# RWKV-6 and a tanh-shrink layer: the own scores of six blocks move from TensorE to VectorE, and the last tile's copies to another buffer

## The chip, the cores and the metric

The kernel runs on one core of one Trainium2 chip. A core has a matrix engine (TensorE, PE in the profile), an elementwise and reduction engine (VectorE, DVE), an engine for scaled copies and functions of one operand (ScalarE, ACT), a general engine (GpSimd, POOL) and a queue that issues most transfers (SyncE, SP). They run side by side, each in its own order, and wait for one another by semaphores. TensorE reads the on-chip memory (SBUF) and writes only PSUM, the small accumulator memory.

The metric is the device time of one execution in microseconds (us). Before the change it is 591.21 us, the median of three runs (590.17 to 591.8).

## The reference

Two layers follow each other. The first is a recurrence over tokens, for each of 4 batches and 8 heads with 48 channels a head and 768 tokens:

```python
for t in range(S):
    kt, vt, rt, wt = (k[:, :, t], v[:, :, t], r[:, :, t], w[:, :, t])
    cur = np.einsum('bhd,bhe->bhde', u[None] * kt, vt)
    y[:, :, t] = np.einsum('bhd,bhde->bhe', rt, state + cur)
    state = wt[:, :, :, None] * state + np.einsum('bhd,bhe->bhde', kt, vt)
```

The second takes the result as x of 3072 rows and 384 columns:

```python
h = x @ w_in            # 384 -> 2048
g = h - np.tanh(h)
return (g @ w_out).astype(np.float32)   # 2048 -> 384
```

What matters here is the part `cur`: token t also sees itself, through the sum over the 48 channels d of r[t,d] u[d] k[t,d], one number for each token and head. This is called the own score of the token. Everything is fp32.

## The kernel before, in words

The 3072 tokens are cut into 8 blocks of 384 tokens (two halves of each batch). The eight heads of a block are four pairs, and two heads lie on the 128 partitions, 64 partitions each of which 48 hold channels. In time a block is cut into six chunks of 64 tokens. Within a chunk, the recurrence becomes matmuls: a 64x64 matrix of scores for each head and chunk, in which the entry (s, t) is what token t takes from token s. Entries with s < t come from k times the decay behind s ("post") and r times the decay before t ("pre"); this phase is `earlier`. Entries with s = t are the own scores; this phase is `own`. Both call `gram`, which makes 48 matmuls of 64x64 for a block (each is two passes in fp32, so 96 rows in the trace), and a masked copy, L406 `copy_predicated`, takes the wanted entries from PSUM into the matrix A (named scores in the profile), twice per phase and block. `own` uses k multiplied by u: `times_u` (L364) does this on ScalarE, four operations a block.

The other phases of a block are: `turn` (transposes), `update` (`update_1` on TensorE makes the contributions of each chunk to the state, `update_2` adds them up on VectorE, ten or eleven small operations at L459 and L469), and the result, in which `from_states` (L510) multiplies pre with the states and `from_scores` (L527) multiplies the scores with v. Scratch in PSUM is a pool of two buffers, `ps_a`, that all phases share; the result takes both.

While the dense layer of block i runs, the phases of block i+1 ("later") are spread over it, and the first scans of block i+2 ("after"). The dense part is a loop over f, 16 slices of 128 of the 2048 inner columns. In each slot f:

- `first` makes hp, six TensorE passes (L668) into a single PSUM buffer, and ScalarE copies it to h (L671).
- `slight` makes g from h. In blocks 2 to 6 ("fast") ScalarE squares (L686, L687, L689) and VectorE does two products (L674). In the other blocks VectorE also does the square (L695).
- `second.add` does the matmuls with w_out. In blocks 2 to 6 it is the class `Fewer` (L775), which multiplies 3x3 tiles with fewer products and needs sums of tiles of g, made on VectorE by `form_g` (L713): one operation in the slot after an even f, four after an odd one. It also needs sums of tiles of w_out, made once by `form_w` (L951): the first half under block 1, the second half under block 2, in slots 4, 6, 8 and 9. The matmuls of slices f-1 and f follow two and three slots after an odd f. Twelve sums (L807) then give the output tiles of a fast block, under the next block, in slots 4, 6, 8 and 9, and `store` sends them off in slot 9, six transfers. In the other blocks the second matmuls are L743.

The order on TensorE, VectorE, ScalarE and SyncE is written out by hand (`manual_schedule`): the order in which the program issues operations is the order on each engine. In a slot, VectorE gets the products of the slot before, the copies of the phase issued in the slot before, the forms, then what the plan prepares, then the weight forms and sums. `plan(i)` is the table of what goes into which slot: `phases` (TensorE phases), `before` (preparations for the later block: `times_behind` L353, `times_before` L346, `held`, `times_u`, `bound`), `ahead` (preparations for the block after: the scans `behind` L339 and `before` L328), and `loads`. A load is tied by `begin_behind` to the copy of h of its slot, and all loads, the stores and the fills of xT go through SyncE's one queue in order. k, r, w and v have one buffer each, which the next load of the same name overwrites.

At the end, the last tile of 128 rows is copied in two halves, by ScalarE and VectorE (L751, L753), into the pool buffer o, which has two buffers used by the two tiles before it (L758), and each half is stored by its own queue.

The table that the change rewrites is this one, for all blocks but block 0:

```python
phases = {4: "own", 6: "earlier", 8: "turn", 10: "update", 12: "result 1"}
...
before.update({4: ("bound 2",), 6: ("bound 0",)})
ahead = {10: ("behind 2", "take_whole 2"), 12: ("behind 0", "take_whole 0"), 13: ("before 2",),
         15: ("before 0",)}
loads = {1: "v", 7: "w", 9: "k", 11: "r"}
```

Of the kernel before, what the change touches and what calls it, by code (L numbers as in the profile page):

```python
# [37 lines left out]
F32 = mybir.dt.float32  # L38
# [13 lines left out]
P = 128  # L52
# [66 lines left out]
def kernel(  # L119
# [4 lines left out]
    wT: bass.AP,  # L124
    v: bass.AP,
    uT: bass.AP,
    weights: bass.AP,
    out: bass.AP,
):
# [12 lines left out]
        nc.vector.memset(shift[:, i:i + 1], value)  # L142
    u_sb = const.tile([P, NPAIR], F32, name="u_sb", tag="u_sb")
    nc.scalar.dma_start(out=u_sb, in_=uT)

    warm = const.tile([P, 1], F32, name="warm", tag="warm")
    nc.scalar.activation(out=warm, in_=shift[:, 0:1], func=AF.Copy)


    seed = const.tile([P, UP * NCH * LP], BF16, name="seed", tag="seed")  # L150
    nc.vector.memset(seed, 0.0)
    nc.vector.memset(seed.rearrange("d (c j) -> d c j", j=LP)[:, :, 0:1], 1.0)


    start = const.tile([P, UP * NCH * LP], F32, name="start", tag="start")
# [66 lines left out]
    fast = range(2, blocks_n - 1)  # L222
    n_whole = blocks_n * NPAIR * NCH
    n_excess, n_top = 2 * blocks_n + len(fast) * NF, (blocks_n - len(fast)) * NF
    holds = const.tile([P, n_whole + n_excess + n_top], F32, name="holds", tag="holds")
    ends = const.tile([P, 3], F32, name="ends", tag="ends")
    excess = const.tile([P, n_excess], F32, name="excess", tag="excess")
    top = const.tile([P, n_top], F32, name="top", tag="top")
# [33 lines left out]
    class Block:  # L262
# [40 lines left out]
        def load(self, name, p0=0, n=NPAIR, as_=None):  # L303
            as_ = as_ or name
            if name == "w":
                dst = self.tile(name)[:, p0 * NCH * LP:(p0 + n) * NCH * LP]
                src = wT[self.b, p0:p0 + n, :, self.q * NCH * LP:(self.q + 1) * NCH * LP]
            else:
                dst = self.tokens(as_, p0, n)
                src = {"r": rT, "k": kT}[name][self.b, p0:p0 + n, :, self.cols]  # L310
            return nc.sync.dma_start(out=dst.rearrange("d (p t) -> d p t", p=n),
                                     in_=src.rearrange("p d t -> d p t"))

        def load_v(self):
            self.v = inp.tile([P, NCP, DM], F32, name="v_sb", tag="v_sb")
# [419 lines left out]
    class Second:  # L735
# [4 lines left out]
        def add(self, f, g):  # L740
            for j in range(NB // P):
                acc = self.acc[j][:, 0:DM]
                nc.tensor.matmul(acc, lhsT=g[:, j * P:(j + 1) * P], rhs=w_out_sb[:, f, :],  # L743
                                 start=(f == 0), stop=(f == NF - 1))
                if f == NF - 1:
                    rows = slice(self.row0 + j * P, self.row0 + j * P + P)
                    if rows.stop == N:
                        for at, engine in ((slice(0, DM // 2), nc.scalar), (slice(DM // 2, DM), nc.vector)):
                            o = dense.tile([P, DM], F32, name="o", tag="o", bufs=2)[:, at]
                            if engine is nc.scalar:  # L750
                                nc.scalar.activation(out=o, in_=acc[:, at], func=AF.Copy, scale=1.0 / UPSCALE)  # L751
                            else:
                                nc.vector.tensor_single_scalar(o, acc[:, at], 1.0 / UPSCALE, op=ALU.mult)  # L753
                            queue = nc.scalar if engine is nc.scalar else nc.sync
                            queue.dma_start(out=out[rows, at], in_=o)
                        continue
                    o = dense.tile([P, DM], F32, name="o", tag="o", bufs=2) if j < 2 else places(12, 3)
                    nc.scalar.activation(out=o, in_=acc, func=AF.Copy, scale=1.0 / UPSCALE)  # L758
                    nc.sync.dma_start(out=out[rows, :], in_=o)
# [57 lines left out]
    def plan(i):  # L817


        converted = ()  # L820
        if i == 0:
            phases = {4: "turn", 6: "update", 8: "own", 11: "earlier", 13: "result 1"}
            before = {0: ("behind 0", "take_whole 0"), 1: ("times_behind 2",), 2: ("times_behind 0",),
                      3: ("before 2",), 4: ("times_u 2",), 5: ("before 0", "times_u 0"), 8: ("times_before", "held")}
            ahead = {14: ("behind 2", "take_whole 2"), 15: ("behind 0", "take_whole 0")}
            converted = range(READY, NF)
            loads = {f: "weights" for f in (0, 1, 3, 4, 5, 6, 7, 8, 9, 10)}
            loads.update({2: "v", 11: "w", 12: "k", 13: "r"})
        else:
            phases = {4: "own", 6: "earlier", 8: "turn", 10: "update", 12: "result 1"}  # L830
            if i == 1:
                before = {0: ("before 2",), 1: ("before 0",), 2: ("times_behind 2", "times_behind 0"),
                          3: ("times_before", "held", "times_u 2", "times_u 0")}
            else:
                before = {0: ("times_behind 2",), 1: ("times_behind 0", "times_u 2"),
                          3: ("times_before", "held", "times_u 0")}
            before.update({4: ("bound 2",), 6: ("bound 0",)})
            ahead = {10: ("behind 2", "take_whole 2"), 12: ("behind 0", "take_whole 0"), 13: ("before 2",),
                     15: ("before 0",)}
            loads = {1: "v", 7: "w", 9: "k", 11: "r"}  # L840
        return phases, before, ahead, converted, loads

    READY = 3
# [5 lines left out]
    def more_weights(queue):  # L849
        raws.append(load_weights(more_weights.n, queue))  # L850
        more_weights.n += 1
        return raws[-1][-1]
# [7 lines left out]
    def boot(ps, blk, later):  # L860
        h1, h2 = HALVES
        for p0 in HALVES:
            for name in ("w", "k", "r"):
                blk.load(name, p0, UP)
        blk.load_v()
        for _ in range(3):
            more_weights(nc.sync)
        ready = []

        def converted():  # L870
            for op in ready.pop(0):
                op()

        both = (h1, h1 + 1), (h2, h2 + 1)
        blk.behind(h1, UP)
        blk.take_whole(h1, UP)
        blk.before(h1, UP)
        blk.times_behind(h1, UP)
        blk.times_u(h1, UP)
        blk.turn(ps, h1)  # L880
        own = blk.own(ps, h1)
        blk.times_before(h1, UP)
        earlier = blk.earlier(ps, h1)
        blk.bound(h1)
        blk.bound(h2)
        blk.behind(h2, UP)
        blk.take_whole(h2, UP)
        blk.times_behind(h2, UP)
        blk.times_u(h2, UP)
        blk.turn(ps, h2)  # L890
        ins = blk.before(h2, UP)
        begin_behind(ins, later.load("w"))
        own()
        own = blk.own(ps, h2)
        blk.times_before(h2, UP)
        earlier()
        blk.update_1(ps)
        own()
        ready.append(convert(*raws.pop(0), halves=True))
        blk.results(ps)  # L900
        blk.result("from_scores", both[0])
        blk.update_2()
        ready.append(convert(*raws.pop(0)))
        later.bound(h1)
        blk.result("from_states", ALL, cs=(0, 1), more=True)
        earlier = blk.earlier(ps, h2)
        blk.result("from_states", ALL, cs=(2,))
        earlier()
        blk.result_out(both[0], True)
        later.bound(h2)  # L910
        blk.fill_holes([nc.sync, nc.scalar, nc.gpsimd])
        more_weights(nc.sync)
        blk.result("from_scores", both[1], True)
        for op in ready[0][0]:
            op()
        ins = blk.result_out(both[1], True, (nc.scalar.copy, nc.vector.tensor_copy))
        begin_behind(ins, more_weights(nc.sync))
        more_weights(nc.sync)
        later.load("k")
        later.load("r")  # L920
        blk.held(0, NPAIR)
        ready[0] = ready[0][1]
        converted()
        ready.append(convert(*raws.pop(0)))
        converted()
        later.prepare("behind 2")
        later.prepare("take_whole 2")
        converted()
# [24 lines left out]
    for i, blk in enumerate(blocks):  # L953
# [14 lines left out]
        for f in range(NF):  # L968
# [29 lines left out]
                    after.prepare(name)  # L998
            if fast and i == 1 and f >= 5 and f - 5 < len(W_FORMS):
                form_w(f - 5, 0)  # L1000
            some = {4: (0, 2), 6: (2, 4), 8: (4, 6), 9: (6, len(SUMS))}.get(f)
            if some and i == fast.start and fast:
                for n in range(some[0], min(some[1], len(W_FORMS))):
                    form_w(n, 4)
            if some and summed:
                summed[0].sum(*some)
                if f == 9:
                    summed.pop().store()
            name, ins = loads.get(f), None
            if name == "weights":  # L1010
                ins = more_weights(nc.sync)
            elif name == "v":
                ins = later.load_v() if later else None
            elif name and after:
                ins = after.load(name)
# [90 lines left out]
```

## Time and profile before

| | |
|---|---|
| median of three runs | 591.21 us (590.17 to 591.8) |
| the profiled execution | 591.68 us, of which the span of the profile is 589.9 us |
| granted TensorE clock | 0.989 |
| VectorE forms L713, 128x256 | 200 operations, 84.8 us, 424 ns each |
| masked copies L406, 128x768 | 32 operations, 30.5 us, 1,005 ns each |
| weight forms L951, 128x512 | 20 operations, 683 to 685 ns each |
| times_before L346, 128x1536 | 7 operations, 1,752 ns each |
| own matmuls L399, r with k | 768 passes over 8 blocks |
| scaling by u, L364 on ScalarE | 32 operations, 17.7 us |
| loads of v, 576 KB | 8, median 4.4 us from issue to landing |
| HBM traffic | 69 GB/s over the span |

The profile is taken of one execution. [...] The chain that ended last is followed back from the last instruction: it says what the end waited for, step by step. A wait is named after what released it. [...]

### The profile page before, as it was taken

What the parts mean: (1) busy time and instruction counts of PE and PEld (TensorE: products, weight loads), DVE (VectorE), ACT (ScalarE), POOL (GpSimd) and SP (SyncE); (2) the same over time, 40 slices, a digit from 0 to 9 for tenths busy, and PEclk for the clock granted to TensorE, in tenths of its full rate; (3) what the DMA queues carried; (4) which work ended last, traced back from release to release, by engine and by line L of the source; (5) the groups of instructions that cost most, each with busy time, mean ns of one, the idle gap of its engine ahead of it and who ended that gap; (6) DMA issues with size and microseconds to landing.
All of it is one profiled execution on the core that took longest, in us unless ns stands there. A gap on an engine that the chain in (4) does not pass through costs nothing.

```text
span 589.9 us, 14756 instructions
## 1 busy us (share of the span) xinstructions
PE 562.6 (95%) x6130; PEld 405.3 (69%) x6130; DVE 455.9 (77%) x906; ACT 343.6 (58%) x689; POOL 10.9 (2%) x39
## 2 busy tenths in 40 slices
PE   3689999999999999999999999999999999999995
PEld 2546656566665787777777787777877787775552
DVE  8899996875877888887887888877888886554541
ACT  4789874343137665587467765686566875532221
POOL 6000000000000000000000000000000000000000
PEclk9789999999999999999999999999999999999998
DMA  8495543202302032011311033011321001000101
GB/s 316 120 388 181 166 159 117 80 2 58 105 12 82 2 109 61 6 42 55 106 56 42 2 96 108 12 42 36 115 66 34 10 1 42 12 1 0 42 1 43
DMA packets 27655, 43.17 MB, mean 73 GB/s; under 512 B 2368, under 2 KB 25536, under 8 KB 27584
## 3 DMA queue, kind: packets, MB, share of 16 engines
q1 hardware_dynamic: 27168, 41.98, 22.0%
q8 instruction: 49, 0.80, 0.6%
q14 instruction: 22, 0.18, 0.1%
q10 hardware_dynamic: 352, 0.15, 0.1%
q0 software_dynamic: 64, 0.05, 0.0%
HBM read 36.28 MB, written 4.72 MB: 69 GB/s over the span
## 4 chain that ended last, share of the span: by engine, by line
PE 89%; DVE 3%; ACT 2%; issue 1%; DMA 0%; DVEq 0%; ACTq 0%
PE hp L668 40%; PE acc L775 19%; PE acc L743 14%; PE att L775 5%; PE att L399 3%; PE att L510 2%; PE att L447 2%; PE att L527 2%; PE att L422 2%; DVE w_sb L251 0%; DVE states L459 0%; ACT up L246 0%; DMA out_y<-o 0%; ACT up L247 0%; DVE states L469 0%
## 5 line engine op out<-in xcount | busy, mean ns | idle before, releaser
L668 PE MATMUL hp<-xT,w_sb 128*128 128x384 f32 x768 | 272.0, 491 | 5.5 <-ACT h L671 3.0
L668 PEld LDWEIGHTS hp<-xT,w_sb 128*128 128x128 f32 x768 | 140.0, 191 | 88.5 <-ACT h L671 7.3
L671 ACT ACTIVATE h<-hp 128x384 f32<-128x384 f32 x128 | 62.7, 490 | 169.6 <-PE hp L668 167.9
L775 PE MATMUL acc<-forms,g 128*128 128x128 f32 x720 | 108.4, 278 | 0.6
L775 PEld LDWEIGHTS acc<-forms,g 128*128 128x128 f32 x720 | 96.2, 192 | 12.8 <-issue 1.2
L713 DVE TENSOR_TENSOR g<-g 128x256 f32<-128x256 f32 x200 | 84.8, 424 | 17.4 <-PE acc L775 1.1
L674 DVE SCALAR_TENSOR_TENSOR h<-h,s 128x384 f32<-128x384 f32 x128 | 70.6, 552 | 25.4 <-ACT s L686 24.9
L674 DVE SCALAR_TENSOR_TENSOR g<-qa,h 128x384 f32<-128x384 f32 x96 | 53.6, 559 | 19.7 <-PE acc L775 8.6
L743 PE MATMUL acc<-w_sb,sums 128*128 128x384 f32 x192 | 68.0, 490 | 0.2
L695 DVE CUSTOM_DVE_ANT_0 s<-h 128x384 f32<-128x384 f32 x48 | 26.7, 555 | 38.3 <-ACT h L671 38.3
L743 PEld LDWEIGHTS acc<-w_sb,sums 128*128 128x128 f32 x192 | 35.7, 190 | 23.7 <-issue 0.5
L687 ACT ACTIVATE qa<-s,shift 128x384 f32<-128x384 f32 x80 | 49.2, 615 | 2.6
L689 ACT ACTIVATE junk<-s,shift 128x384 bf16<-128x384 f32 x80 | 47.9, 599 | 0.0
L686 ACT ACTIVATE s<-h 128x384 f32<-128x384 f32 x80 | 41.9, 524 | 2.5
L698 ACT ACTIVATE qa<-s,shift 128x384 f32<-128x384 f32 x48 | 29.5, 614 | 23.9 <-DVE top L695 23.9
L775 PE MATMUL acc<-w_sb,g 128*128 128x128 f32 x240 | 39.9, 275 | 0.0
L743 PE MATMUL acc<-w_sb,g 128*128 128x384 f32 x96 | 33.3, 487 | 0.0
L775 PEld LDWEIGHTS acc<-w_sb,g 128*128 128x128 f32 x240 | 33.2, 192 | 0.0
L406 DVE COPY_PREDICATED scores<-mask_all,att 128x768 f32<-128x768 uint8 x32 | 30.5, 1005 | 1.4 <-PE att L399 1.4
L328 DVE TENSOR_TENSOR_SCAN pre<-w,start 128x780 f32<-128x780 f32 x16 | 28.6, 1786 | 0.6
L339 DVE TENSOR_TENSOR_SCAN post<-w,seed 128x780 f32<-128x780 f32 x16 | 28.4, 1776 | 0.0
L775 PE MATMUL att<-w_sb,g 128*128 128x128 f32 x160 | 26.8, 275 | 0.0
(80 smaller groups left out, 537.7 us busy)
## 6 DMA issues: line engine op xcount, KB each, us to landing
raw<-in_weights SPq DMA_DIRECT2D x16, 768.0 KB, 5.2
w<-in_wT SPq DMA_DIRECT2D x7, 780.0 KB, 4.4
k<-in_kT SPq DMA_DIRECT2D x7, 768.0 KB, 4.7
r<-in_rT SPq DMA_DIRECT2D x7, 768.0 KB, 4.6
v_sb<-in_v SPq DMA_DIRECT2D x8, 576.0 KB, 4.4
out_y<-sums SPq DMA_DIRECT2D x15, 128.0 KB, 1.9
out_y<-o SPq DMA_DIRECT2D x6, 192.0 KB, 2.5
xT<-late SPq DMA_DIRECT2D x44, 24.0 KB, 1.9
```

Of the source, the lines that this page charges most:

```text
L328: return nc.vector.tensor_tensor_scan(out=self.tile("pre")[:, cols], data0=self.tile("w")[:, cols], data1=start[:, 0:n * NCH * LP], initia ...
L406: return lambda: nc.vector.copy_predicated(out=A[:, :, p0:p0 + UP].rearrange("s h p c t -> s h (p c) t"), mask=mask.to_broadcast([P, 2, UP ...
L668: nc.tensor.matmul(hp, lhsT=w_in_sb[:, f, kc, :], rhs=xT[kc], start=(kc == KC - 1), stop=(kc == 0))
L671: return h, nc.scalar.activation(out=h, in_=hp, func=AF.Copy, scale=1.0 / UPSCALE)
L674: return lambda: nc.vector.scalar_tensor_tensor(out=out, in0=in0, scalar=scalar, in1=in1, op0=op0, op1=ALU.mult)
L686: nc.scalar.activation(out=s, in_=h, func=AF.Square)
L687: nc.scalar.activation(out=qa, in_=s, func=AF.Square, bias=shift[:, 4:5])
L689: nc.scalar.activation(out=junk[:, 0:NB], in_=s, func=AF.Relu, bias=shift[:, 5:6], accum_out=excess[:, at:at + 1])
L698: first = [lambda: nc.scalar.activation(out=qa, in_=s, func=AF.Square, bias=shift[:, 4:5])]
L713: return lambda: nc.vector.tensor_tensor(out=G[:, to:to + 2], in0=two(G, g_at(q, a0), g_at(q, a1)), in1=two(G, g_at(q, b0), g_at(q, b1)), ...
L743: nc.tensor.matmul(acc, lhsT=g[:, j * P:(j + 1) * P], rhs=w_out_sb[:, f, :], start=(f == 0), stop=(f == NF - 1))
L775: nc.tensor.matmul(to, lhsT=G[:, g_at(q, a), :], rhs=rhs, start=start, stop=stop, skip_group_check=True)
```

## The change

Three things are changed.

First, in the phases of blocks 2 to 7 (those that run under the dense part of blocks 1 to 6) the own phase is gone, and with it `times_u`. In its place k and r are loaded a second time, now with tokens on partitions (128 tokens, three groups of 128, 384 = 8 x 48 columns), into the same buffers k and r once their channel form has been used. VectorE multiplies k by u (`product_u`, a row of u that is the same on all partitions), then by r (`product_r`), sums over the 48 channels of each head (`product_sum`) into a small tile `diagonal`, and two masked copies (`diagonal_in`) spread the sums over the diagonal of A. Blocks 0 and 1 keep the phase of matmuls. The host gives two more arrays, tokens and u_all.

Second, the plan is moved: earlier from slot 6 to 4, turn from 8 to 7. The weight forms under block 2 go by twos in slots 4, 6, 8, 9 and 10; the output sums are 2, 2, 2, 2 in slots 4, 6, 8 and 9, the last four in slot 14, and the six stores with them.

Third, the two halves of the last tile are copied into a place in the tile sums (places 12 to 14), where the third tile of other blocks is copied too. Besides, two constants become narrower: seed from bf16 to uint8, holds from fp32 to bf16.

```diff
+    u_row = const.tile([P, DM], F32, name="u_row", tag="u_row")
+    diagonal = const.tile([P, 2, NPAIR, NCP], F32, name="diagonal", tag="diagonal")
...
-    seed = const.tile([P, UP * NCH * LP], BF16, name="seed", tag="seed")
+    seed = const.tile([P, UP * NCH * LP], U8, name="seed", tag="seed")
...
-    holds = const.tile([P, n_whole + n_excess + n_top], F32, name="holds", tag="holds")
+    holds = const.tile([P, n_whole + n_excess + n_top], BF16, name="holds", tag="holds")
...
+        def by_token(self, name):
+            return self.tile(name)[:, 0:NCP * DM].rearrange("t (c e) -> t c e", c=NCP)
+
+        def load_tokens(self, name):
+            src = tokens["kr".index(name), self.b, self.q * NB:(self.q + 1) * NB]
+            return nc.sync.dma_start(out=self.by_token(name), in_=src.rearrange("(c t) e -> t c e", t=P))
+
+        def product_u(self, p0, n):
+            t = self.by_token("k")
+            nc.vector.tensor_tensor(out=t, in0=t, in1=u_row.unsqueeze(1).to_broadcast([P, NCP, DM]), op=ALU.mult)
+
+        def product_r(self, p0, n):
+            t = self.by_token("k")
+            nc.vector.tensor_tensor(out=t, in0=t, in1=self.by_token("r"), op=ALU.mult)
+
+        def product_sum(self, p0, n):
+            src = self.by_token("k").rearrange("t c (p h d) -> t c p h d", p=NPAIR, h=2)
+            nc.vector.tensor_reduce(out=diagonal.rearrange("t h p c -> t c p h"), in_=src, op=ALU.add,
+                                    axis=mybir.AxisListType.X)
+
+        def diagonal_in(self, p0, n):
+            mask = masks["diagonal"].bitcast(U8).unsqueeze(1).unsqueeze(1)
+            data = diagonal[:, :, p0:p0 + n].rearrange("s h p c -> s h (p c)").unsqueeze(3)
+            nc.vector.copy_predicated(
+                out=A[:, :, p0:p0 + n].rearrange("s h p c t -> s h (p c) t"),
+                mask=mask.to_broadcast([P, 2, n * NCP, L]), data=data.to_broadcast([P, 2, n * NCP, L]))
...
-                            o = dense.tile([P, DM], F32, name="o", tag="o", bufs=2)[:, at]
+                            o = places(12, 3)[:, at]
...
-            phases = {4: "own", 6: "earlier", 8: "turn", 10: "update", 12: "result 1"}
+            phases = {4: "earlier", 7: "turn", 10: "update", 12: "result 1"}
             if i == 1:
                 before = {0: ("before 2",), 1: ("before 0",), 2: ("times_behind 2", "times_behind 0"),
-                          3: ("times_before", "held", "times_u 2", "times_u 0")}
+                          3: ("times_before", "held")}
             else:
-                before = {0: ("times_behind 2",), 1: ("times_behind 0", "times_u 2"),
-                          3: ("times_before", "held", "times_u 0")}
-            before.update({4: ("bound 2",), 6: ("bound 0",)})
+                before = {0: ("times_behind 2",), 1: ("times_behind 0",), 3: ("times_before", "held")}
+            before.update({4: ("bound 2",), 5: ("product_u",), 6: ("bound 0", "product_r"), 7: ("product_sum",),
+                           8: ("diagonal_in 2",), 9: ("diagonal_in 0",)})
...
-            loads = {1: "v", 7: "w", 9: "k", 11: "r"}
+            loads = {1: "v", 3: "tokens k", 4: "tokens r", 7: "w", 9: "k", 11: "r"}
...
+        nc.sync.dma_start(out=u_row, in_=u_all)
...
-            some = {4: (0, 2), 6: (2, 4), 8: (4, 6), 9: (6, len(SUMS))}.get(f)
-            if some and i == fast.start and fast:
-                for n in range(some[0], min(some[1], len(W_FORMS))):
-                    form_w(n, 4)
+            some = {4: (0, 2), 6: (2, 4), 8: (4, 6), 9: (6, 8), 14: (8, len(SUMS))}.get(f)
+            of = {4: 0, 6: 2, 8: 4, 9: 6, 10: 8}.get(f)
+            if i == fast.start and fast and of is not None:
+                form_w(of, 4)
+                form_w(of + 1, 4)
             if some and summed:
                 summed[0].sum(*some)
-                if f == 9:
+                if some[1] == len(SUMS):
                     summed.pop().store()
...
+            elif name and name.startswith("tokens"):
+                ins = later.load_tokens(name[-1]) if later else None
```

## The prediction, made before the changed kernel was run

> **What bounds the kernel now.** I read, in this order, the page (busy times, the chain that ended last), the chain in order of time, VectorE's timeline, and the timeline of the tail. PE, DVE, ACT and SP are TensorE, VectorE, ScalarE and the queue of SyncE; a slot is one turn of the loop over f, and i is the number of the block whose dense part runs.
>
> ```profile
> PE 562.6 (95%) x6130; PEld 405.3 (69%) x6130; DVE 455.9 (77%) x906; ACT 343.6 (58%) x689; POOL 10.9 (2%) x39
> ...
> PE 89%; DVE 3%; ACT 2%; issue 1%; DMA 0%; DVEq 0%; ACTq 0%
> ```
>
> TensorE works 562.6 of 589.9 us and is 89% of the chain. So TensorE time removed from the stages shown next is time saved, until another engine holds TensorE up. The chain in order of time (start, us, what) shows what one phase costs:
>
> ```profile
> 227.51 1.56 PE att L510 x96
> ...
> 258.07 1.94 PE hp L668 x6
> 260.00 1.56 PE att L399 x96
> 263.10 1.94 PE hp L668 x6
> 266.37 1.94 PE hp L668 x6
> ```
>
> With the own phase, one hp starts 263.10 - 258.07 = 5.03 us after the one before; the slot after it, without a phase, takes 266.37 - 263.10 = 3.27. An own phase so costs 1.76 us, more than its 1.56, since the switches to and from it cost 0.2. In block 1 slots of 5.63 and 3.87 give 1.76 too. VectorE's timeline (start, us, line) is the other half:
>
> ```profile
> 339.00 0.56 DVE L674 SCALAR_TENSOR_TENSOR g<-qa,h 128x384 f32<-128x384 f32 x1 [0.36 <-PE acc L775]
> 339.47 1.90 DVE L406 COPY_PREDICATED scores<-mask_all,att 128x768 f32<-128x768 uint8 x2
> 341.26 0.41 DVE L713 TENSOR_TENSOR g<-g 128x256 f32<-128x256 f32 x1
> 342.40 0.56 DVE L674 SCALAR_TENSOR_TENSOR h<-h,s 128x384 f32<-128x384 f32 x1 [0.73 <-ACT s L686]
> 343.06 0.56 DVE L674 SCALAR_TENSOR_TENSOR g<-qa,h 128x384 f32<-128x384 f32 x1
> 343.66 2.02 DVE L713 TENSOR_TENSOR g<-g 128x256 f32<-128x256 f32 x4
> 345.59 0.88 DVE L807 TENSOR_TENSOR sums<-sums 128x256 f32<-128x256 f32 x2
> 346.38 0.55 DVE L674 SCALAR_TENSOR_TENSOR h<-h,s 128x384 f32<-128x384 f32 x1
> ```
>
> VectorE runs one group per slot: h and g of the slot before, that slot's copies, its forms (one or four), then what the plan adds. The starts give the pitch: h 0.66, g 0.47 ahead of copies, 0.66 ahead of one form, 0.59 ahead of four; two copies 1.79; one form 0.35; four forms 1.93; two sums 0.80. The bracketed waits (0.36, 0.73) are its slack here. It is 77% busy over the kernel, but over a steady block nearly full (summed below).
>
> [...]
>
> **The change part by part.**
>
> *Own phases, -10.56 us.* Six go, one under each of blocks 1 to 6: 6 x 1.76 = 10.56. The earlier phase moves from slot 6 to 4 and turn from 8 to 7; they cost the same there. The 24 ScalarE scalings by u (605 ns each, about 14.5 us) go too, worth nothing: ScalarE waits 169.6 us for hp in all.
>
> *New VectorE work.* Per block two products and one reduce of 1,152 elements. [...] The two copies of the own scores stay two, now from SBUF; I take 0.93 for one alone (in a pair 0.90; bounds 0.85 and 1.0).
>
> *Does it fit?* A steady block before, by pitch: eight slot pairs (h, g, one form 1.67; h, g, four forms 3.18) 38.8; four scans 7.7; times_behind 2 x 0.87; times_before and held 1.75; sums 4.65; states 11 x 0.39 = 4.2; four copies 3.6; others_summed 0.5. Together 62.9 of a block's 67.9 (hp to hp, 263.10 to 331.04). After: 62.9 + 3.8 + 0.1 = 66.8 against TensorE's 67.9 - 1.8 = 66.2. VectorE is full, but it may run late: its forms are ready 2 to 6 us before their matmuls (374.77 for 376.75, 353.79 for 359.95). So what counts is where the lateness meets a deadline. The nearest is the start of from_states in slot 12, whose PSUM buffers are those that the states' last add must have read.
>
> *Steady blocks 3 to 6.* Groups 5 to 10, after: 4.54, 5.25, 2.94, 4.91, 3.40, 5.08, together 26.12 (group 5: h, g, two copies, form, product_u = 0.66+0.47+1.79+0.35+1.27). In block 4, h of slot 4 starts at 329.81; +26.12, h and g 1.13, ten states operations 3.9 gives 360.96. from_states started at 363.32, now 1.76 earlier: 361.56. It just fits, with 0.6 to spare; before it had 1.1. The last four sums go to slot 14, which adds 1.56 there, and waits of 1.45 and 0.34 in the next slots 1 and 2 take up nearly all of it. About 0.3 stays, so the spare is 0.3. I charge 0.2 a block, 0.8 (bounds 0 and 4, the latter at 1.7 us per new operation, 1.3 more a block less the spare).
>
> *Block 2.* Here VectorE also makes ten weight forms (0.61 each) where steady blocks do sums, and two of these move from slot 9 to 10.
>
> ```profile
> 194.86 0.55 DVE L674 SCALAR_TENSOR_TENSOR h<-h,s 128x384 f32<-128x384 f32 x1
> ```
>
> ```profile
> 222.42 0.35 DVE L459 TENSOR_TENSOR states<-states,whole 128x192 f32<-128x192 f32 x1
> ...
> 226.31 0.36 DVE L459 TENSOR_TENSOR states<-states,whole 128x192 f32<-128x192 f32 x1
> ```
>
> Groups 5 to 10: 4.54, 5.67, 2.94, 5.33, 3.82, 6.30, together 28.60. 194.86 + 28.60 + 1.13 + 3.9 = 228.5 for the last add. from_states could start at 227.51 - 1.76 = 225.75. TensorE waits 2.8 us (bounds 2 and 4). The wait of slot 11's matmuls for the two late weight forms lies inside these 2.8. Queued behind it on TensorE is everything; nothing later makes it up. Block 1 has waits of about 1.5 us a slot on VectorE ahead of its squares, which hide each product: no charge.
>
> *Tail.* The timeline of the end:
>
> ```profile
> 584.31 0.33 ACT L751 ACTIVATE o<-acc 128x192 f32<-128x192 f32 x1 [1.37 <-DMA out_y<-o]
> 584.67 0.37 ACTq L755 DMA_DIRECT2D out_y<-o  x1
> 584.95 0.36 DVE L753 TENSOR_SCALAR o<-acc 128x192 f32<-128x192 f32 x1 [7.21 <-DMA out_y<-o]
> 585.33 0.33 SPq L755 DMA_DIRECT2D out_y<-o  x1
> ```
>
> ScalarE's and VectorE's halves of the last tile wait for stores of the o buffers they reuse. With a place in sums they can start when the last matmul ends: 582.43 (the chain) + 0.65 = 583.1, so the last store is issued at about 583.5, 1.8 earlier. Two stores then overlap the 192 KB one of 1.88 us; I take -1.6 (bounds -1.0 and -1.85). The sums there must have been stored: slot 14's sums end near 574.5, six stores take 2.87 to issue and 1.9 to land, about 579.3. That leaves 3.8.
>
> *Transfers.* Twelve loads of 576 KB, like v's (4.4 us to landing). k is issued behind h of slot 3 (324.71 in block 4) and lands by 329.6; product_u starts near 333. r follows times_before and h of slot 4 (328.5), lands by 333.3, is needed near 337.5. So hidden by 3 to 4 us; without cover a late one would cost TensorE as much as it is late beyond VectorE's spare. The six stores moved to slot 14 pass the loads of k and r and the xT rows on SP, which go earlier; they are issued by 380, ahead of v's load at 386.0. u_row adds 192 KB at the start, where DMA is 80 to 90% busy: +0.2 (0 to 0.5). The narrower seed and holds only make room: nothing.
>
> Sum: -10.56 + 2.8 + 0.8 - 1.6 + 0.2 = -8.4. The profiled execution took 591.68 (span 589.9 and 1.8 around it), 0.47 over the median 591.21; it gives 583.3, the median 582.8. I forecast 582.8.
>
> **The rivals.** *A: VectorE's lateness costs nothing (10%).* If its pitches are short or TensorE's waits are cut finer than I take them, block 2 pays under 1 us and the steady ones nothing: -10.56 - 1.8 + 0.8 = 579.7. For it: idle time remains in every block. Against: ten weight forms plus two products in six slots. *B: VectorE becomes the bound, still faster (20%).* At 1.55 us per new operation instead of 1.27 each block carries 0.84 more: block 2 waits 2.8 + 0.8 = 3.6, blocks 3 to 6 some 0.6 each (0.84 less the spare), and the tail gives 1.0: 591.2 - 10.56 + 3.6 + 2.4 - 1.0 + 0.3 = 585.9. For it: 66.8 against 66.2. *C: slower than before (8%).* Only the new operations can do it. Past the spare, each us per block is paid in full in blocks 2 to 6. To eat 8.4 us they must grow by 1.7 + 0.3 us a block, to 1.93 each; above that it is slower. At 2.2 us, 2.8 more a block, block 2 pays 2.8 and the four others 2.5 each over the spare: 582.8 + 2.8 + 10.0 - 0.8 = 594.8. [...] *D: no change (2%)*, 1.9 us each.
>
> **How the numbers follow.** Forecast 60%, A 10, B 20, C 8, D 2. The forecast's own range is 581 to 585; taking in most of A and B, 579.5 to 587. A measurement of this kernel tells 0.3%, 1.8 us, from no change: faster 0.90, same 0.02, slower 0.08.
>
> **What would show it.** The profile after should have no own matmuls in blocks 1 to 6 and slots without them; products near 1.36 us and a reduce near 1.35; one TensorE wait of about 3 us ahead of from_states (released by VectorE's states) in block 2, and under 0.5 in others; the last store issued within 1 us of the last matmul. Waits of 1 us or more in every block speak for B; a product waiting for a transfer would refute my cover.

## The result, and the profile after

The changed kernel takes 582.13 us (median of four runs, 580.06 to 583.34); the kernel before took 591.5 beside it. The ratio is 0.984, with a 95% interval of 0.981 to 0.987. In a later set the changed kernel took 582.95 and the one before 590.17, a ratio of 0.987 (0.984 to 0.989). The forecast was 582.8, in a range from 579.5 to 587. The profiled execution took 581.84, its span is 580.1.

The page of the changed kernel, busy times and the chain that ended last:

```profile
PE 554.4 (96%) x5554; PEld 398.1 (69%) x5554; DVE 476.6 (82%) x924; ACT 331.6 (57%) x665; POOL 10.8 (2%) x39
...
PE 85%; DVE 5%; ACT 4%; issue 0%; DVEq 0%
```

TensorE is busy 8.2 us less, VectorE 20.7 us more. In the chain TensorE falls from 89 to 85% and VectorE grows from 3 to 5%, but that says little of the change: the kernel with the tail alone, below, has 85 and 4% too.

The best single view is one that no row gives ready: the starts of the first hp pass of each block on TensorE's timeline, and their differences. The block numbers are those of the dense part, i. For block 2 these are the lines of before and then of after (the second line of each is the start of block 3):

```profile
175.73 2.10 PE L668 MATMUL hp<-xT,w_sb 128*128 128x384 f32 x6
...
242.12 2.10 PE L668 MATMUL hp<-xT,w_sb 128*128 128x384 f32 x6
```

```profile
172.23 2.10 PE L701 MATMUL hp<-xT,w_sb 128*128 128x384 f32 x6
...
240.84 2.10 PE L701 MATMUL hp<-xT,w_sb 128*128 128x384 f32 x6
```

All blocks, in us:

| block | before | after | difference |
|---|---|---|---|
| 1 | 72.13 | 70.37 | -1.76 |
| 2 | 66.39 | 68.61 | +2.22 |
| 3 | 67.95 | 66.18 | -1.77 |
| 4 | 68.01 | 66.18 | -1.83 |
| 5 | 67.95 | 66.19 | -1.76 |
| 6 | 67.93 | 66.18 | -1.75 |

So five of the six blocks give about the 1.76 of an own phase, and one block is slower than before. The new operations, grouped by form (duration in us of all, mean ns of one):

```profile
L343 DVE COPY_PREDICATED scores<-mask_all,diagonal 128x768 f32<-128x768 uint8 x12 | 12.2, 1016 | 0.0
L328 DVE TENSOR_TENSOR k<-k,u_row 128x1152 f32<-128x1152 f32 x6 | 8.1, 1352 | 0.0
L332 DVE TENSOR_TENSOR k<-k,r 128x1152 f32<-128x1152 f32 x6 | 8.1, 1351 | 0.0
L336 DVE TENSOR_REDUCE diagonal<-k 128x24 f32<-128x1152 f32 x6 | 8.1, 1347 | 0.0
```

The prediction expected products near 1.36 us and a reduce near 1.35; they take 1,351 and 1,352 ns, and 1,347. In a steady block (block 4) VectorE's timeline starts h of slot 4 and ends the states, here their last add, at:

```profile
326.77 0.55 DVE L707 SCALAR_TENSOR_TENSOR h<-h,s 128x384 f32<-128x384 f32 x1
...
357.61 0.35 DVE L502 TENSOR_TENSOR states<-states,att 128x192 f32<-128x192 f32 x1
```

and TensorE's timeline of the same block has:

```profile
356.49 2.10 PE L701 MATMUL hp<-xT,w_sb 128*128 128x384 f32 x6
358.52 1.63 PE L543 MATMUL att<-pre,states 48*64 48x64 f32 x96
```

From h to the start of the last add are 30.84 us; that add lasts 0.35 and the buffers are free at 357.96. from_states starts at 358.52, straight behind hp: 0.56 us to spare, no wait. In block 2 VectorE's timeline has the same two points further apart:

```profile
190.91 0.55 DVE L707 SCALAR_TENSOR_TENSOR h<-h,s 128x384 f32<-128x384 f32 x1
...
224.12 0.35 DVE L502 TENSOR_TENSOR states<-states,att 128x192 f32<-128x192 f32 x1
```

33.21 us to the start of the last add, 33.56 to its end; the walk of the prediction gave 28.60 + 1.13 + 3.9 = 33.63. Here TensorE waits. Its timeline of slot 12, with waits in brackets:

```profile
219.91 2.10 PE L701 MATMUL hp<-xT,w_sb 128*128 128x384 f32 x6
223.84 0.33 PE L543 MATMUL att<-pre,states 48*64 48x64 f32 x4 [1.83 <-DVE states L502]
224.62 1.62 PE L543 MATMUL att<-pre,states 48*64 48x64 f32 x92 [0.45 <-DVE states L502]
226.32 1.04 PE L808 MATMUL acc<-forms,g 128*128 128x128 f32 x4
...
229.00 1.98 PE L560 MATMUL att<-scores,v_sb 64*48 64x64 f32 x96
230.91 1.56 PE L701 MATMUL hp<-xT,w_sb 128*128 128x384 f32 x4
```

The first four passes of from_states use the buffer that is free first; they start 1.83 us late, and the others wait 0.45 more for the last add. The same slot in the kernel before:

```profile
225.41 2.10 PE L668 MATMUL hp<-xT,w_sb 128*128 128x384 f32 x6
...
229.18 0.71 PE L775 MATMUL acc<-forms,g 128*128 128x128 f32 x4
...
232.20 2.20 PE L668 MATMUL hp<-xT,w_sb 128*128 128x384 f32 x6
```

Then comes something that the prediction did not have. From the first pass of the second product to the next hp, through 12 passes of the second product and the 96 of from_scores, the slot takes 4.59 us (226.32 to 230.91) where it took 3.02 (229.18 to 232.20). The stretches show why (busy time of PE, PEld, DVE, ACT, POOL; then the granted clock, the DMA share and GB/s):

```profile
222.00:224.00 2.00, 0.17 (x5) 0.19 (x4) 1.83 (x6) 1.89 (x4) 0.00 (x0) 1.00 0.43 162
224.00:226.00 2.00, 1.55 (x95) 1.44 (x93) 1.83 (x6) 0.34 (x2) 0.00 (x0) 1.00 0.00 0
226.00:228.00 2.00, 1.92 (x23) 1.79 (x13) 1.65 (x5) 0.00 (x0) 0.00 (x0) 0.63 0.05 12
228.00:230.00 2.00, 2.00 (x46) 1.78 (x48) 2.00 (x2) 0.00 (x0) 0.00 (x0) 0.51 0.00 0
230.00:232.00 2.00, 2.00 (x72) 1.52 (x65) 1.73 (x6) 1.28 (x4) 0.00 (x0) 1.00 0.00 0
```

From 226 to 230 us, right after the wait, TensorE runs at 0.63 and 0.51 of its clock. Slot 12 takes 11.0 us in place of 6.79. Of the 4.2 more, 2.6 are the wait, with what the two interruptions cost beside their 2.28 of idle time (hp to second product: 6.41 for 3.77), and 1.6 the clock (4.59 for 3.02).

The tail, in the timeline of all engines:

```profile
574.06 0.49 ACT L791 ACTIVATE o<-acc 128x384 f32<-128x384 f32 x1 [0.15 <-PE acc L776]
574.71 0.33 ACT L784 ACTIVATE sums<-acc 128x192 f32<-128x192 f32 x1 [0.15 <-PE acc L776]
...
575.07 0.36 DVE L786 TENSOR_SCALAR sums<-acc 128x192 f32<-128x192 f32 x1 [5.72 <-ACT sums L784]
575.88 0.40 SPq L788 DMA_DIRECT2D out_y<-sums  x1
```

No half waits for a store any more. The copy of the second tile in the kernel before:

```profile
582.46 0.49 ACT L758 ACTIVATE o<-acc 128x384 f32<-128x384 f32 x1 [0.15 <-PE acc L743]
```

Before, the last store was issued 2.87 us after this copy started (582.46 to 585.33), now 1.82 after it (574.06 to 575.88). From that copy to the end of the span it was 7.4 us and is now 6.0.

### The profile page after: what moved, and what is told of

Its sections match the earlier page's. It is cut to its first block, busy times and chain, and to the rows that moved or that the text cites. A ratio compares the mean times of both kernels' runs of the same rounds, so it can differ in the third digit from the quotient of the medians.

```text
span 580.1 us, 13603 instructions
## 1 busy us (share of the span) xinstructions
PE 554.4 (96%) x5554; PEld 398.1 (69%) x5554; DVE 476.6 (82%) x924; ACT 331.6 (57%) x665; POOL 10.8 (2%) x39
## 4 chain that ended last, share of the span: by engine, by line
PE 85%; DVE 5%; ACT 4%; issue 0%; DVEq 0%
PE hp L701 40%; PE acc L808 19%; PE acc L776 13%; PE att L808 5%; PE att L543 2%; PE att L432 2%; PE att L560 2%; PE att L480 2%; PE att L455 1%; ACT up L250 1%; DVE w_sb L255 1%; ACT up L251 1%; ACT w_sb L247 1%; DVE states L492 1%; DVE states L502 1%
## 5 line engine op out<-in xcount | busy, mean ns | idle before, releaser
L707 DVE SCALAR_TENSOR_TENSOR sums<-qa,h 128x384 f32<-128x384 f32 x32 | 17.9, 558 | 11.1 <-ACT qa L731 7.6
```

The source lines that it names most:

```text
L707: return lambda: nc.vector.scalar_tensor_tensor(out=out, in0=in0, scalar=scalar, in1=in1, op0=op0, op1=ALU.mult)
```

## The experiments

The block times of all kernels, read as above (us):

| kernel | block 1 | 2 | 3 | 4 | 5 | 6 |
|---|---|---|---|---|---|---|
| before | 72.13 | 66.39 | 67.95 | 68.01 | 67.95 | 67.93 |
| after | 70.37 | 68.61 | 66.18 | 66.18 | 66.19 | 66.18 |
| after, once more | 70.38 | 68.62 | 66.38 | 66.22 | 66.18 | 66.18 |
| forms spread | 70.37 | 64.89 | 66.18 | 66.20 | 66.19 | 66.18 |
| sum twice | 70.38 | 69.92 | 67.12 | 67.13 | 67.48 | 66.18 |
| own back | 72.13 | 66.39 | 67.95 | 67.93 | 67.94 | 67.94 |
| second product first | 70.37 | 65.54 | 66.75 | 66.31 | 66.19 | 66.17 |
| forms early, own buffer | 70.37 | 64.20 | 66.21 | 66.26 | 66.23 | 66.18 |
| operations beside own | 72.13 | 67.36 | 67.94 | 67.94 | 67.94 | 67.94 |

### The tail alone

The kernel before with the one edit:

```diff
-                            o = dense.tile([P, DM], F32, name="o", tag="o", bufs=2)[:, at]
+                            o = places(12, 3)[:, at]
```

> The kernel before with one part of the change alone: the two halves of the last tile are copied into places 12 to 14 of sums. Theory (a stall of the tail removed): the last store is issued about 1 us earlier behind the last copy of ScalarE for the second tile, and the span from that copy to the end falls from 7.4 to about 6.0 us; the whole is 1.4 us less, about 590.0. Rival (the end is set by the flight of the 192 KB store, so an earlier issue is worth nothing): under 0.3 us.

Measured: 588.22 us beside 590.01, a ratio of 0.9973 (0.9963 to 0.9983), so 1.6 us less (1.0 to 2.2). Its tail:

```profile
580.30 0.49 ACT L758 ACTIVATE o<-acc 128x384 f32<-128x384 f32 x1 [0.15 <-PE acc L743]
...
580.95 0.33 ACT L751 ACTIVATE sums<-acc 128x192 f32<-128x192 f32 x1 [0.15 <-PE acc L743]
...
581.31 0.36 DVE L753 TENSOR_SCALAR sums<-acc 128x192 f32<-128x192 f32 x1 [5.72 <-ACT sums L751]
581.69 0.33 SPq L755 DMA_DIRECT2D out_y<-sums  x1
```

The last store is issued 1.39 us after the second tile's copy starts (580.30 to 581.69), against 2.87 before, and the span ends 5.9 after it. The theory holds, the rival doesn't. One thing is left: VectorE's half starts only when ScalarE's ends (5.72 <-ACT). That was put down to both halves lying in sums; a later run shows otherwise.

### The own matmuls back

```diff
-            phases = {4: "earlier", 7: "turn", 10: "update", 12: "result 1"}
+            phases = {4: "own", 6: "earlier", 8: "turn", 10: "update", 12: "result 1"}
...
-            before.update({4: ("bound 2",), 5: ("product_u",), 6: ("bound 0", "product_r"), 7: ("product_sum",),
-                           8: ("diagonal_in 2",), 9: ("diagonal_in 0",)})
+            before.update({4: ("bound 2",), 6: ("bound 0",)})
...
-            loads = {1: "v", 3: "tokens k", 4: "tokens r", 7: "w", 9: "k", 11: "r"}
+            loads = {1: "v", 7: "w", 9: "k", 11: "r"}
```

and times_u again in `before` of all blocks.

> The kernel after with the own phases of blocks 2 to 7 back as matmuls (own in slot 4, earlier in 6, turn in 8, the scaling by u on ScalarE, no token loads, no products, no diagonal copies of sums); the moved weight forms and output sums, the narrower constants, the load of u_row and the tail stay. Theory (the own matmuls are the gain): blocks 3 to 6 take 67.9 to 68.0 us again, block 2 has no wait over 0.5, and only the tail's 1.4 and what the start gives are left: about 589.5. Rival (a good part of the gain comes from the moved plan, or from the start, where the profile of after runs 1.7 us ahead by the end of block 0): 586 to 588.

Measured: 588.15 us, a ratio of 0.9971 (0.9962 to 0.998), the same as with the tail alone (588.22, 0.9973). In microseconds this is nearer to the rival's figures, since the kernel before took 590.0 in this set; the ratio and the block times decide. Block by block it is the kernel before again. So the own phase is the whole gain of blocks 1 and 3 to 6, and the moved weight forms and sums, the narrower constants and the load of u_row cost nothing that can be seen here. The rival falls.

### The weight forms spread over block 2

```diff
-            of = {4: 0, 6: 2, 8: 4, 9: 6, 10: 8}.get(f)
-            if i == fast.start and fast and of is not None:
-                form_w(of, 4)
-                form_w(of + 1, 4)
+            of = {0: range(0, 3), 1: range(3, 5), 2: range(5, 6), 4: range(6, 7), 6: range(7, 8), 8: range(8, 9),
+                  9: range(9, 10)}.get(f, ())
+            if i == fast.start and fast:
+                for n in of:
+                    form_w(n, 4)
```

> The kernel after, with the ten weight forms under block 2 made three, two, one, one, one, one and one in slots 0, 1, 2, 4, 6, 8 and 9 instead of by twos in slots 4, 6, 8, 9 and 10. Theory (the wait of TensorE ahead of from_states in block 2 is VectorE's backlog of weight forms on top of the new products, and the lower granted clock of 0.79 that follows comes from that wait): slot 12 of block 2 falls from 11.0 to about 6.8 us, the clock there is 1.0, and the kernel takes about 577.7, 4.4 less than after. Rival 1 (the lower clock comes at that time whatever TensorE waits for): the wait of 2.3 goes, but the slow passes stay, about 579.8. Rival 2 (the wait comes from the phases that moved a slot or two, not from the forms): nothing changes, 582.

Measured: 578.45 us, 0.75 over the expected figure, a ratio of 0.9804 (0.9788 to 0.982). Slot 12 of block 2 on TensorE's timeline, and the clock there:

```profile
219.98 2.10 PE L701 MATMUL hp<-xT,w_sb 128*128 128x384 f32 x6
222.01 0.33 PE L543 MATMUL att<-pre,states 48*64 48x64 f32 x4
222.67 1.62 PE L543 MATMUL att<-pre,states 48*64 48x64 f32 x92 [0.33 <-DVE states L502]
```

```profile
222.00:226.00 4.00, 3.59 (x115) 3.22 (x118) 3.48 (x9) 2.23 (x5) 0.00 (x0) 1.00 0.33 119
226.00:230.00 4.00, 4.00 (x108) 3.13 (x109) 3.72 (x7) 2.01 (x5) 0.00 (x0) 1.00 0.07 15
```

The wait shrinks to 0.33 and the clock stays at 1.00; slot 12 takes 7.4 us, not quite the expected 6.8, and block 2 falls by 3.7. Both rivals fall: moving the forms alone takes away all but 0.33 of the wait, and the slow passes go with it.

### The second product ahead of from_states

```diff
-                if f in phases:
+                if f in phases and (i, f) != (fast.start, 12):
                     behind += later.phase(ps_a, phases[f])
...
+            if later and (i, f) == (fast.start, 12):
+                behind += later.phase(ps_a, "result 1")
             if later and phases.get(f) == "result 1":
```

> The kernel after with one thing moved: in slot 12 of block 2 the slot's 12 passes of the second product (1.34 us) come ahead of from_states instead of behind it, so that TensorE has work in part of its wait; VectorE is as late as before. Theory (a wait of 2 us lowers the clock, one of 1 us or less doesn't, as the waits of 0.7 us with the doubled reduce didn't): TensorE's wait falls to about 1.0, the clock stays 1.0, slot 12 takes about 8.0 us in place of 11.0, and the kernel is 2.5 to 3 us faster than after. Rival (any wait there is followed by the slow passes): slot 12 takes about 9.7, the gain is 1.3.

Measured: 580.19 us, a ratio of 0.982 (0.980 to 0.984), beside 582.95 for the changed kernel in the same set: 2.8 less. TensorE's timeline of the slot, and the stretches:

```profile
221.23 2.10 PE L701 MATMUL hp<-xT,w_sb 128*128 128x384 f32 x6
223.17 0.61 PE L808 MATMUL acc<-forms,g 128*128 128x128 f32 x4
...
225.16 0.33 PE L543 MATMUL att<-pre,states 48*64 48x64 f32 x4 [0.49 <-DVE states L502]
225.94 1.62 PE L543 MATMUL att<-pre,states 48*64 48x64 f32 x92 [0.45 <-DVE states L502]
```

```profile
222.00:226.00 4.00, 3.07 (x25) 2.27 (x25) 3.65 (x12) 2.40 (x7) 0.00 (x0) 1.00 0.50 184
226.00:230.00 4.00, 3.89 (x191) 3.41 (x192) 3.55 (x9) 1.05 (x3) 0.00 (x0) 1.00 0.02 6
```

VectorE is as late as before, but with 1.34 us of work put into the gap the waits are 0.49 and 0.45, the clock stays at 1.00, and the slot takes 7.92 us; the expectation said 8.0. Of the 3.1 saved in the slot, 1.5 is the shorter wait, filled with the moved work, and 1.6 is the clock that was not lost. Block 3 is 0.57 longer in this execution than in the changed kernel's; TensorE waits for no other engine there, and its one pause, of 0.30 in from_scores, has no cause in the profile.

### The changed kernel once more

> The changed kernel once more, beside the others of this call, for its own block times: the wait of about 2.3 us in slot 12 of block 2 and the granted clock near 0.5 for some 4 us after it should come again if they belong to the kernel and not to one execution; about 581 us where the kernel before takes 590.

Measured: 582.95 us. Slot 12 of block 2 takes 11.0 us again, with the same waits of 1.8 and 0.5 and a clock of 0.55 and 0.59 in the two stretches behind. It belongs to the kernel. Block 3 is 0.2 longer here, with no wait on any engine. This run also settles where the two profiled executions differed ahead of block 1, which began at 103.60 before and at 101.86 after: here it begins at 103.68, with the same kernel. In the first 50 us the clock is 0.50 for a time that differs from one execution to the next: in all 6.8 us in the profile of after, 13.7 in this run and 10.2 in the kernel before. Over all ten profiles of this document it is between 3.4 and 13.7 us, and the longer it is, the later block 1 begins, from 101.17 (3.4, the reduce made twice) to 103.68 (this run).

So 1.7 us of the difference between the two profiles (9.8 us) is no effect of the change.

### The reduce made twice

```diff
-            before.update({4: ("bound 2",), 5: ("product_u",), 6: ("bound 0", "product_r"), 7: ("product_sum",),
+            before.update({4: ("bound 2",), 5: ("product_u",), 6: ("bound 0", "product_r"), 7: ("product_sum", "product_sum"),
```

(the second makes the same sums again)

> The kernel after with the reduce over channels made twice (the same numbers again), 1.27 us more of VectorE in each of blocks 1 to 6. Theory (VectorE's spare in a steady block is about 0.7 us ahead of from_states and its whole idle time there 0.3 us): block 2 grows by about 1.3, blocks 3 to 6 by 0.6 to 1.2 each, and from_states waits in each of them; 4 to 6 us in all, 586 to 588, more if each wait is followed by a lower clock as in block 2. Rival (VectorE has room, and the block 2 wait is an event of its own): blocks 3 to 6 keep 66.2 us, and at most block 2 grows: 582 to 583.5.

Measured: 587.83 us, a ratio of 0.996 (0.995 to 0.998). Who waited for whom (us in total, times, longest), then the stretch behind the wait in block 4, the wait in block 5, and the stretch behind the wait in block 2:

```profile
PE att L543 <- DVE states L502: 4.4, 5, 1.8
...
PE acc L808 <- DVE forms L985: 1.2, 1, 1.2
```

```profile
361.00:367.00 6.00, 5.84 (x204) 5.14 (x205) 5.51 (x11) 2.86 (x8) 0.00 (x0) 1.00 0.06 19
```

```profile
428.56 1.62 PE L543 MATMUL att<-pre,states 48*64 48x64 f32 x92 [1.01 <-DVE states L502]
```

```profile
226.00:228.00 2.00, 1.92 (x65) 1.74 (x56) 1.76 (x4) 0.00 (x0) 0.00 (x0) 0.57 0.01 4
```

Block 2 grows by 1.3, blocks 3 to 5 by 0.9, 0.9 and 1.3; block 6, which prepares only block 7 and makes no scans for a block behind it, doesn't grow. Of 1.27 us added, 0.3 were free in blocks 3 and 4 and nothing in block 5. That is VectorE's spare in a steady block, and it is about what the prediction had worked out (0.3). The rival falls.

The waits of blocks 3 to 5 (0.65, 0.65 in two pieces, and 1.01) leave the clock at 1.00 in this execution. In block 2 the wait of the changed kernel is there again, 1.82 and 0.45, and the low clock behind it too; the 1.3 that the block grows is a further wait ahead of it, for the weight forms. This profile is of the fastest of 17 executions, and the others lie up to 4 us above it. Their clock over the whole run was 0.982 to 0.987 in twelve of the thirteen above 587 us, and 0.989 to 0.995 in the four below. So the longer ones had the lower clock; whether it was lower at the start or behind these waits is open, since they have no profile.

### The operations beside the own matmuls

The kernel with the own matmuls back, and with the operations two slots later than in the change, since the own matmuls still need k and r in slot 4:

```diff
-            before.update({4: ("bound 2",), 6: ("bound 0",)})
+            before.update({4: ("bound 2",), 6: ("bound 0",), 7: ("product_u",), 8: ("product_r",),
+                           9: ("product_sum",)})
...
-            loads = {1: "v", 7: "w", 9: "k", 11: "r"}
+            loads = {1: "v", 5: "tokens k", 6: "tokens r", 7: "w", 9: "k", 11: "r"}
```

> The kernel with the own matmuls back (as in the run before) that also loads the tokens and makes the two products and the reduce in slots 7, 8 and 9, whose sums are not used: VectorE's new work without TensorE's gain. Theory (the operations cost nothing where TensorE sets the pace and only meet a deadline in block 2): blocks 3 to 6 keep 67.9 us, block 2 waits some 0.7 us, in all 0.5 to 1.5 us more than without them, 588.7 to 589.6. Rival (the operations or their loads slow other work by themselves, over a shared memory or a queue): blocks 3 to 6 grow too, 2 us or more in all.

Measured: 589.94 us, 0.3 over the expected range, a ratio of 0.999 (0.998 to 1.000), where the tail alone, in another set, had 0.997: about 1.1 us more. Nearly all of it is in block 2, 0.97 us; the waits there:

```profile
PE att L543 <- DVE states L502: 0.6, 2, 0.4
```

Blocks 3 to 6 keep 67.94. So the operations and their loads take nothing from others; only the same deadline in block 2 is missed, by 0.6, and slot 12 takes 7.75. With TensorE slower by 1.76 a block nearly the same VectorE work costs 1.0 in block 2 (67.36 for 66.39) in place of 4.0, and nothing in the others. The cost of the change on VectorE is the meeting of two things, its added work and TensorE's earlier arrival.

### The forms early, and a buffer of its own for VectorE's half

```diff
                             o = places(12, 3)[:, at]
+                            if engine is nc.vector:
+                                o = G[:, 0:3].rearrange("p t c -> p (t c)")[:, at]
...
-            of = {4: 0, 6: 2, 8: 4, 9: 6, 10: 8}.get(f)
-            if i == fast.start and fast and of is not None:
-                form_w(of, 4)
-                form_w(of + 1, 4)
+            of = {(1, 4): (0, 1), (1, 7): (2, 3), (2, 0): (4, 5), (2, 1): (6,), (2, 2): (7,), (2, 6): (8,),
+                  (2, 8): (9,)}.get((i, f), ())
+            if fast:
+                for n in of:
+                    form_w(n, 4)
```

> The kernel after with the ten weight forms of block 2 placed where VectorE waits: two each in slots 4 and 7 of block 1, then two, one, one, one and one in slots 0, 1, 2, 6 and 8 of block 2; and VectorE's half of the last tile in a buffer of its own (three tiles of g), since with both halves in sums it waited for ScalarE's. Theory: block 1 keeps 70.4 us, block 2 falls to about 64.3 (66.4 before, less 1.76 and 0.4), no wait ahead of from_states, and the last store is issued 0.3 us earlier: about 577.5 to 578 where the kernel before takes 590, faster than both. Rival (VectorE late in block 1 now delays its squares and products): block 1 grows by up to 1 us and nothing is won over the spread forms (578.4).

Measured: 578.11 us, a ratio of 0.981 (0.978 to 0.984). Block 1 keeps its 70.37, block 2 takes 64.20, the expected 64.3, and slot 12 is back at 6.79 without a wait. As a time it can't be told from the forms spread (578.45). The second half of the edit missed:

```profile
570.22 0.33 ACT L786 ACTIVATE sums<-acc 128x192 f32<-128x192 f32 x1 [0.15 <-PE acc L776]
...
570.58 0.36 DVE L788 TENSOR_SCALAR g<-acc 128x192 f32<-128x192 f32 x1 [5.72 <-ACT sums L786]
```

VectorE's half still starts when ScalarE's ends, 5.72 us after its last work, though it now writes to another tile. So the shared tile sums was not the reason. In all three tails shown both halves read one accumulator (acc, 128x192 each), and VectorE's starts 0.36 us behind ScalarE's, which lasts 0.33 (574.71 to 575.07 in the changed kernel, 580.95 to 581.31 with the tail alone, 570.22 to 570.58 here). Two accumulators were not tried, so why one half waits for the other was not shown.

## Why the prediction was right, and where a step of it was not

- *Own phases, -10.56.* Right. Blocks 1 and 3 to 6 lose 1.75 to 1.83 us each, and with the own phase back the blocks are those of before.
- *The price of the new operations.* Right: 1.35 us each, start to start 1.27 (330.24 to 331.51). The single copies last 1.02 and take 0.91 from start to start, for 0.93. The 1.27 us that the sums of the prediction take for a new operation (3.8 for the three of a block), and the 1.36 us it expected for a product, were its author's estimate: no run made before it shows them, and the changed kernel shows 1.27 from start to start, 1,351 and 1,352 ns for the two products and 1,347 for the reduce. A straight line through two sizes of the trace before, 424 ns for 256 elements and 1,752 for 1,536, would have given an estimate of 1,354 for 1,152.
- *Steady blocks, +0.8.* The mechanism was right, the charge too high. In none of blocks 3 to 6 did TensorE wait for VectorE, in either execution of the changed kernel; in the second block 3 grew by 0.2 for another reason. Taking a fifth of a microsecond a block for a thin spare was a hedge, not a reading. The spares that stood beside it were good: 0.6 ahead of from_states was 0.56, and 0.3 over the block is what the doubled reduce showed in two blocks of three.
- *Block 2, +2.8.* The place, the cause and the wait were right: the waits of 1.83 and 0.45 cost 2.6, and the weight forms 0.2 in slot 11, which the prediction had inside its 2.8. What failed is that the step counted the wait alone. After it TensorE's clock was 0.50 for 3.4 us, which cost 1.6 more. Against that, slot 2 became 0.44 shorter (2.68 for 3.12): before, two scalings of k stood on ScalarE ahead of the next copy of h, for which TensorE waited 1.03 us, and 0.58 after. The prediction held the scalings to be worth nothing because ScalarE waits 169.6 us in all, and a sum over the kernel doesn't show such a place. So the term is +2.22 + 1.76 = 4.0 in place of 2.8.
- *Tail, -1.6.* Right: -1.4 between the profiles, -1.6 alone. That VectorE's half would wait for ScalarE's was not seen, nor that SyncE would still be issuing the two stores before (573.93 to 575.78): the last store came 1.2 us behind the last matmul, not within 1.
- *u_row, +0.2.* Can't be told: the start differs by 1.8 us between two executions of one kernel. In the profiles with 6.8 us of low clock block 1 begins at 101.53 without u_row (one profile) and at 101.63 to 102.05 with it (four), which is no proof of anything near 0.2.
- *Transfers.* Right as far as waits show: none for tokens is among them.

The sum with the measured terms: -10.56 + 4.0 + 0.1 - 1.5 = -8.0, against 8.4 forecast and 9.4 and 7.2 between the medians of the two sets; the profiles differ by 9.8, and without the 1.7 of the start by 8.1. That the forecast came so near is in part luck: a clock that wasn't thought of (1.6 too little) was offset by a charge for steady blocks that wasn't due (0.7 too much), by slot 2 (0.4) and by u_row (up to 0.2).

The rivals: A had no cost in block 2, and block 2 is where the cost is. B, VectorE as the bound in each block, is what the doubled reduce makes; the change itself stops 0.3 us short of it. C and D would have needed operations half as long again as they are.

## What to carry to other kernels

Before work goes from the bound engine to one that is 77% busy, sum that engine's work for one steady period and then walk its order up to the nearest point where the bound engine must wait for it; do the walk again for each period that differs, since here one block with ten extra operations took back 4 of the 10.6 us. Where such a wait can't be removed, put work that is ready into it: 1.34 us moved ahead of the wait saved 2.8 here, since the clock then stayed at 1.00, where it had been 0.63 and 0.51. And add the tail on its own account: two copies that waited for a store were worth nearly as much as one block's phase (1.6 and 1.76).

## What the runs showed of the hardware

TensorE's granted clock fell after a wait, not in it (1.00 from 222 to 226 us in the changed kernel, 0.63 and 0.51 in the 4 us after). Behind waits of 1.8 and 0.45 us, with four passes between, it was 0.50 for 3.4 us in three profiled executions (two of the changed kernel, one with the reduce made twice), and that cost 1.5 to 1.6 us beside the 2.6 of the wait. It fell 1.9, 1.8 and 1.0 us after the last of the two waits had ended, so not at a fixed distance behind it. Behind waits of 0.5 and 0.45 in the same place, and of 0.65 to 1.01 us in blocks 3 to 5 of another kernel, it stayed at 1.00, each in one profiled execution. So 2.3 us of waiting in two pieces were followed by the lower clock, and 0.95 in two pieces or 1.01 in one were not; whether the length of the wait decides, or when it falls, was not shown.
